# A three-stage fp32 kernel on one core: token sums of two blocks move to GpSimd, and kept products move ahead of a block's last units

## The chip, the cores and the metric

One core of a Trainium2 chip runs the whole program. The metric is the device time in microseconds of one execution, taken as the median over runs. Lower is better. The engines are TensorE (PE, with its weight loads as PEld), VectorE (DVE), ScalarE (ACT), GpSimd (POOL) and SyncE (SP), whose queue issues every DMA here.

## What is computed

Attention over 4 batches, 8 heads, 576 tokens and 64 columns (4 heads with a local mask, 4 with a strided one), then a maxout layer, then a second layer with a leaky activation:

```
x = attention(q, k, v)                                   # 2304 tokens x 512
x = max(x @ w1, x @ w2, x @ w3) @ w_out                  # 512 -> 768 -> 512
h = x @ w_in                                             # 512 -> 2048
out = (max(h, 0) + alpha * min(h, 0)) @ w_out2           # 2048 -> 512
```

## The kernel before, in words

Every fp32 operand of a matmul is kept as two parts, a high part (rounded to fp32r) and a low part (what the rounding left). A product is then three matmuls: high by high, low by high, high by low. `split` (L201) makes the two parts: the high one on ScalarE (L203), the low one by a subtraction (L206).

**First stage** (up to about 394 us). Attention and the maxout layer of batches 0 to 2 are written as tasks, and a planner (`Weave`) sets the order of the instructions. The maxout layer of the last batch is written by hand in `first_net`: 36 gate units of 12 matmuls each (L542), then 8 output units of 18 matmuls (L564). Its result goes to memory by the stores of L575.

**Second stage** (from about 395 us). The 2304 tokens are three blocks of 768, each block two halves of 384. Both products of the second layer are done with 7 block products where 8 would be usual, so sums and differences of the token rows are needed first. `load_x2` (L669) reads a half's rows, `sum_x2` (L677) makes four differences of 128x384, and `split_x2` makes high and low parts of the seven operands of that half. For block 0 this is done at the end of `first_net` and the parts stay on chip. For blocks 1 and 2 it is done early by the generator `early_x2`, whose parts are stored to memory (`xd`, L697) and fetched when the block begins (L704). The generator for block 1 runs beside `first_net`, one step in each of its 44 units `n`. The one for block 2 runs beside the pairs `n` = 1 to 15 of the second stage. In both, DVE does the differences and the low parts.

In the second stage a pair `n` (8 pairs `q` = 0 to 7 in a block) is seven products of the first matrix (`h_products`, L959) on two PSUM banks `ph`, `a` and `b_` in turn. DVE adds each bank up with what came before (L964) before the bank is written again. ACT and DVE then apply the activation (L916, L917, L920), make sums (L946) and split the four results `gts` (L795 on ACT, L796 on DVE). The products with the second matrix are units of 3 matmuls (`o_products`, L802): 12 units (`o_units`, `k` = 0 to 3, three units each) on six banks `po`, run one pair later between the `h_products`. Three more sums of each pair are kept (tiles `k`). After the last pair of a block their products are run: three groups `k` of eight pairs `p`, three units each (`kept_units`), which need `prepare` (split of a kept tile, ACT then DVE) first. `quarter` adds finished banks to the output and stores it.

Order around the block's end before: after the last `h_products` come two units of the pair before, then the nine units `k` = 0, 1, 2 of the last pair, then the kept products `p` = 0, 1 on the two `ph` banks, then the units `k` = 3, then all other kept products. `prepare` runs two ahead of its use:

```
for k in range(4):
    if q == NQ - 1 and k == 3:
        banks = [ps_h.tile(...) for _ in range(2)]
        for p in range(2):
            prepare(blk)
            yield from kept_units(blk, 0, p, banks, ...)
```

PSUM has eight banks. `ps_h` (two) is opened before `ps_o` (six), on the banks that `first_net` used.

Of the kernel before, what the change touches and what calls it, by code (L numbers as in the profile page):

```python
# [10 lines left out]
F32 = mybir.dt.float32  # L11
# [10 lines left out]
P = 128  # L22
# [19 lines left out]
NOW = 9  # L42

# [114 lines left out]
def attention_maxout_prelu_kernel(  # L158
# [523 lines left out]
    def split_x2(blk, k, i, pool, tag):  # L682

        t = pool.tile([P, 2, HB], F32R, tag=tag, name=tag)
        split(t[:, 0], t[:, 1], xs.pop((blk, PRODUCTS[k][1], i)), nc.scalar, nc.vector)
        return t

    def early_x2(blk, gap=0, rest=0):

        for i in range(2):  # L690
            rows = load_x2(blk, i, xsp, "xs")
            for _ in range(1 + gap):
                yield
            sum_x2(blk, i, rows, nc.vector)
            for k in range(7):
                t = split_x2(blk, k, i, xst, "xst")
                nc.sync.dma_start(xd[blk][k][i], t.bitcast(F32))  # L697
                for _ in range(1 + rest):
                    yield
# [53 lines left out]
    xst = pool(ctx, "xst", 2, "right")  # L753
    for n in range(2):
        load_h(n, (0, 2, 1, 3))
    early = early_x2(1, 2, 1)
    for n, _ in enumerate(first_net(B - 1, GATES_LAST)):
        if n in range(20, 32) and (n - 20) * 3 // 4 > (n - 21) * 3 // 4:
            load_ow()
        next(early, None)  # L760
        if n == LOAD_X:
            assert next(early, None) is None
# [5 lines left out]
        for i in range(2):  # L768
            if n == SPLIT_X + 2 * i:
                if i:  # L770
                    sum_x2(0, 1, rows[1], nc.vector)
                for k in range(7):
                    x2h[0, k, i] = split_x2(0, k, i, xmp, f"x{k}{i}")
# [7 lines left out]
    osp = pool(ctx, "osp", 3)  # L781
    ps_h = ctx.enter_context(tc.tile_pool(name="ps_h", bufs=2, space=PSUM, reuse_waits="tile"))
    ps_o = ctx.enter_context(tc.tile_pool(name="ps_o", bufs=6, space=PSUM, reuse_waits="tile"))
# [59 lines left out]
    def o_units(n):  # L843
        blk, q = divmod(n, NQ)
        for k in range(4):
            if q == NQ - 1 and k == 3:

                banks = [ps_h.tile([P, DM], F32, tag="ph", name="ph") for _ in range(2)]
                for p in range(2):
                    prepare(blk)  # L850
                    yield from kept_units(blk, 0, p, banks, parts_.pop((blk, 0, p)))
            w = words[blk, "o1", q, k // 2]
            for t in range(3):
# [10 lines left out]
                yield  # L864
        if q < NQ - 1:
            return
        for k in range(3):
            if k:
                banks = [ps_o.tile([P, DM], F32, tag="po", name="po") for _ in range(2)]
            for p in range(0 if k else 2, NQ):  # L870
                prepare(blk)
                yield from kept_units(blk, k, p, banks, parts_.pop((blk, k, p)))

    def kept_units(blk, k, p, banks, g):
        w = words[blk, "o2", k, p // 2]
        for t in range(3):
# [7 lines left out]
            while drains and (t == 2 or k == 2 and p == NQ - 1):  # L884
                quarter(*drains.pop(0))
                if len(drains) % 2 == 0 and p < NQ - 1:
                    break
# [60 lines left out]
    def h_products(n):  # L948
# [17 lines left out]
        a, b_ = banks  # L966
# [44 lines left out]
    early = early_x2(2)  # L1011
    outs = iter(())
    for n in range(NQ * NBLK):
# [9 lines left out]
        for i, _ in enumerate(h_products(n)):  # L1023
            if q == NQ - 1 and blk + 1 < NBLK:
                fetch_x2(blk + 1, i)
            if i == 0 and 0 < n < 16 and n != 8:
                for _ in range(2 if q in (5, 6) else 1):
                    next(early, None)
# [59 lines left out]
```

## Time and profile before

| what | value |
|---|---|
| median of 3 runs | 764.44 us (764.08 to 765.48) |
| profiled execution, first to last instruction | 762.9 us |
| around that span (median less span) | 1.5 us |
| PE busy | 741.8 us, 97% |
| DVE busy | 596.8 us, 78% |
| ACT busy | 454.7 us, 60% |
| POOL busy | 3.2 us, in 16 instructions |
| DMA | 199.37 MB, mean 261 GB/s |

The profiled execution's own time beside its span is not listed separately; the span is what the trace shows, and the sum in the prediction is made against it. Busy shares are averages over the stages. PE's is modelled from pipelined matmuls, so that small waits between weight loads can hide in it: counts of matmuls over a stretch say more than the busy time.

### The profile page before, as it was taken

How to read it: one execution, taken by the hardware profiler on the slowest of the kernel's cores; microseconds unless marked ns; L12 is line 12 of the kernel's file. 1: busy time of each engine (PE TensorE's matmuls, PEld its weight loads, DVE VectorE, ACT ScalarE, POOL GpSimd, SP SyncE). 2: the span in 40 equal slices, each digit the busy share in tenths (PEclk: the TensorE clock that was granted, in tenths of full speed). 3: DMA queues.
4: the chain of work that ended last, by engine and by line, in shares of the span. 5: the costliest groups of instructions: out<-in, count | busy, mean ns of one | idle time of the engine just before them, and what ended most of it. 6: DMA issues, size and time to landing. Idle time of an engine off the chain costs nothing.

```text
span 762.9 us, 16093 instructions
## 1 busy us (share of the span) xinstructions
PE 741.8 (97%) x5704; PEld 723.0 (95%) x5704; DVE 596.8 (78%) x1670; ACT 454.7 (60%) x1226; POOL 3.2 (0%) x16
## 2 busy tenths in 40 slices
PE   5899999999999999999999999999999999999997
PEld 4699999999999999999999999999999999999997
DVE  5999999888777987336368988878888877888894
ACT  6988897756665775323246566624666644566561
POOL 1000000000000000000000000000000000000000
PEclk9699999999999999999999999999999999999999
DMA  7387769877878856566938889999888999878361
GB/s 245 130 259 232 240 216 326 271 273 255 300 248 282 270 202 213 171 259 192 362 113 285 273 289 320 386 403 334 291 285 301 354 401 328 273 239 259 121 194 59
DMA packets 85471, 199.37 MB, mean 261 GB/s; under 512 B 10640, under 2 KB 40848, under 8 KB 85392
## 3 DMA queue, kind: packets, MB, share of 16 engines
q1 hardware_dynamic: 85392, 198.35, 75.9%
q8 instruction: 45, 0.74, 0.4%
q14 instruction: 34, 0.28, 0.1%
HBM read 148.51 MB, written 49.81 MB: 260 GB/s over the span
## 4 chain that ended last, share of the span: by engine, by line
PE 77%; DVE 12%; DMA 5%; ACT 2%; issue 2%; SPq 1%; DVEq 0%; ACTq 0%
PE bank L542 27%; PE ph L959 20%; PE po L802 15%; PE bank L564 9%; PE bank L314 3%; PE bank L380 2%; PE bank L355 2%; DVE g L796 2%; DVE c L806 2%; DMA w<-wh 1%; DMA w<-wp 1%; DVE e L322 1%; DMA xs<-x 1%; DMA x<-xd 1%; DVE c L964 1%
## 5 line engine op out<-in xcount | busy, mean ns | idle before, releaser
L542 PE MATMUL bank<-x,w 128*128 128x288 f32 x1728 | 236.5, 297 | 0.3 <-DVE t L553 0.3
L542 PEld LDWEIGHTS bank<-x,w 128*128 128x128 f32 x1728 | 231.1, 189 | 2.1 <-DVE t L553 0.6
L959 PE MATMUL ph<-x,w 128*128 128x384 f32 x1008 | 203.4, 337 | 1.8 <-DVE c L964 1.2
L802 PE MATMUL po<-w,g 128*128 128x256 f32 x1296 | 183.8, 282 | 1.7 <-DVE g L796 0.8
L802 PEld LDWEIGHTS po<-w,g 128*128 128x128 f32 x1296 | 175.4, 189 | 4.2 <-DVE g L796 3.2
L959 PEld LDWEIGHTS ph<-x,w 128*128 128x128 f32 x1008 | 168.3, 188 | 3.0 <-DVE c L964 1.9
L964 DVE TENSOR_TENSOR c<-ph,c 128x384 f32<-128x384 f32 x168 | 91.0, 554 | 32.7 <-PE ph L959 31.8
L795 ACT CAST g<-c 128x384 fp32r<-128x384 f32 x96 | 48.5, 505 | 89.7 <-DVE c L946 53.0
L564 PE MATMUL bank<-h,w 128*128 128x288 f32 x576 | 79.9, 297 | 0.4 <-DVE nm L322 0.4
L564 PEld LDWEIGHTS bank<-h,w 128*128 128x128 f32 x576 | 76.9, 188 | 1.8 <-DVE nm L322 0.8
L250 DVE TENSOR_TENSOR w<-word,w 128x512 fp32r<-128x512 f32 x88 | 55.4, 637 | 23.9 <-ACT w L247 23.5
L329 ACT ACTIVATE e<-e,nm 96x128 f32<-96x128 f32 (+2 forms) x176 | 68.0, 394 | 6.0 <-DVE nm L322 6.0
L916 ACT ACTIVATE c<-c 128x384 f32<-128x384 f32 x96 | 50.5, 526 | 33.9 <-DVE c L964 32.9
L247 ACT CAST w<-word 128x512 fp32r<-128x512 f32 x88 | 50.6, 582 | 32.0 <-DMA wh<-w 17.7
L917 ACT ACTIVATE c<-c,nalpha 128x384 f32<-128x384 f32 x96 | 59.2, 617 | 3.1
L920 DVE SCALAR_TENSOR_TENSOR c<-c 128x384 f32<-128x384 f32 x96 | 53.0, 552 | 9.0 <-ACT c L917 9.0
L796 DVE TENSOR_TENSOR g<-c,g 128x384 fp32r<-128x384 f32 x96 | 52.9, 551 | 1.9 <-ACT g L795 1.9
L796 DVE TENSOR_TENSOR g<-k,g 128x384 fp32r<-128x384 f32 x72 | 36.8, 550 | 14.4 <-ACT g L795 14.4
L439 ACT ACTIVATE word<-raw 128x512 f32<-128x512 f32 x56 | 37.4, 677 | 11.5 <-DMA raw<-in_w 5.9
L445 DVE SCALAR_TENSOR_TENSOR word<-raw,word 128x512 uint32<-128x512 uint32 x56 | 38.8, 693 | 1.9
L631 DVE TENSOR_TENSOR t<-bank,t 128x288 f32<-128x288 f32 x72 | 32.6, 452 | 7.8 <-PE bank L542 7.1
L795 ACT CAST g<-k 128x384 fp32r<-128x384 f32 x72 | 33.4, 515 | 7.8 <-PE po L802 4.4
(72 smaller groups left out, 679.8 us busy)
## 6 DMA issues: line engine op xcount, KB each, us to landing
w<-wh SPq DMA_DIRECT2D x72, 512.0 KB, 5.0
raw<-in_w SPq DMA_DIRECT2D x50, 512.0 KB, 4.5
w<-wo SPq DMA_DIRECT2D x48, 512.0 KB, 5.9
w<-wp SPq DMA_DIRECT2D x36, 512.0 KB, 6.3
wh<-w SPq DMA_DIRECT2D x24, 512.0 KB, 3.7
xd<-xst SPq DMA_DIRECT2D x28, 384.0 KB, 3.5
x<-xd SPq DMA_DIRECT2D x28, 384.0 KB, 8.1
wp<-w SPq DMA_DIRECT2D x24, 256.0 KB, 3.0
```

The lines of the kernel that those rows point to most:

```text
L247: (nc.scalar.copy if e == "ACT" else nc.vector.tensor_copy)(out_, in_)
L250: nc.vector.tensor_tensor(out=out_, in0=x, in1=y, op=ALU.subtract)
L329: nc.scalar.activation(tl[ek][:nq, j, i, :nk], tl[ek][:nq, j, i, :nk], AF.Exp, bias=tl["nm", u][:nq, j, i:i + 1], scale=-1.0, accum_out=tl ...
L542: nc.tensor.matmul(acc, words["gate", f, g][:, wi, cc * P:(cc + 1) * P], xt[b, cc, hf][:, xi, :], start=n == 0, stop=n == 3 * NCC - 1)
L564: nc.tensor.matmul(acc, words["mix", f][:, wi, dc * P:(dc + 1) * P], st["h", hf, f][:, xi, :], start=n == 0, stop=n == 3 * NF1 - 1)
L795: nc.scalar.copy(g[:, 0], x)
L796: return g, lambda: nc.vector.tensor_tensor(out=g[:, 1], in0=x, in1=g[:, 0].bitcast(F32), op=ALU.subtract)
L802: nc.tensor.matmul(bank[:, NH * half:NH * (half + 1)], g[:, gi, t * P:(t + 1) * P], w[:, wi, off:off + NH], start=first and i == 0, stop=l ...
L917: nc.scalar.activation(a, a, AF.Copy, scale=nalpha[:, f:f + 1])
L920: nc.vector.scalar_tensor_tensor(out=a, in0=h, scalar=0.0, in1=a, op0=ALU.max, op1=ALU.add)
L959: nc.tensor.matmul(bank, words["h", n, i][:, wi, off + c * P:off + (c + 1) * P], x2h[blk, k, c][:, xi, :], start=m == 0, stop=m == 5)
L964: nc.vector.tensor_tensor(out=out_, in0=bank, in1=other, op=ALU.add)
```

## The change

1. The differences and low parts of blocks 1 and 2 go from DVE to GpSimd (`lo_engine=nc.gpsimd`, `sum_x2(..., nc.gpsimd)`). High parts stay on ACT. They are 16 differences and 28 low parts, each 128x384.
2. The rows of both halves of block 1 are loaded ahead of the first eight weight loads `wh`, the second half into a pool `xr` of its own.
3. The steps of both blocks stand in tables by `n`, and the store of a part is issued a step later than its split.
4. For block 0 the second half's differences and splits are written one unit apart.
5. `ps_o` is opened before `ps_h`, and the seven products begin on the other bank (`b_, a = banks`).
6. The kept products `p` = 0, 1 run ahead of all twelve units of the last pair. `prepare` then runs after units 1, 2 and 3, and up to five ahead (`AHEAD`). Finished banks are added at most two at a time.

```diff
+EARLY = 6
-    def split_x2(blk, k, i, pool, tag):
+    def split_x2(blk, k, i, pool, tag, lo_engine=nc.vector):
-        split(t[:, 0], t[:, 1], xs.pop(...), nc.scalar, nc.vector)
+        split(t[:, 0], t[:, 1], xs.pop(...), nc.scalar, lo_engine)
-    def early_x2(blk, gap=0, rest=0):
...
+    def early_load(blk, i, pool, tag):
+        early_rows[blk, i] = load_x2(blk, i, pool, tag)
+    def early_sums(blk, i):
+        sum_x2(blk, i, early_rows.pop((blk, i)), nc.gpsimd)
+    def early_split(blk, i, k):
+        early_parts.append((blk, k, i, split_x2(blk, k, i, xst, "xst", nc.gpsimd)))
+    def early_store():
+        for blk, k, i, t in early_parts:
+            nc.sync.dma_start(xd[blk][k][i], t.bitcast(F32))
+        early_parts.clear()
...
+    xrp = pool(xrx, "xr", 2, "right")
+    early_load(1, 0, xsp, "xs")
+    early_sums(1, 0)
+    early_load(1, 1, xrp, "xr")
     for n in range(2):
         load_h(n, (0, 2, 1, 3))
-    early = early_x2(1, 2, 1)
+    ready = {EARLY + 19 * j // 10: divmod(j, 7) for j in range(14)}
     for n, _ in enumerate(first_net(B - 1, GATES_LAST)):
-        next(early, None)
+        if n - 1 in ready:
+            early_store()
+        if n in ready:
+            if ready[n] == (1, 0):
+                early_sums(1, 1)
+            early_split(1, *ready[n])
...
-    ps_h = ctx.enter_context(tc.tile_pool(name="ps_h", bufs=2, ...))
     ps_o = ctx.enter_context(tc.tile_pool(name="ps_o", bufs=6, ...))
+    ps_h = ctx.enter_context(tc.tile_pool(name="ps_h", bufs=2, ...))
...
     def o_units(n):
+        if q == NQ - 1:
+            first = [ps_h.tile([P, DM], F32, tag="ph", name="ph") for _ in range(2)]
+            for p in range(2):
+                yield from kept_units(blk, 0, p, first, parts_.pop((blk, 0, p)))
         for k in range(4):
-            if q == NQ - 1 and k == 3:
...
+            if q == NQ - 1 and k > 0:
+                prepare(blk)
...
             for p in range(0 if k else 2, NQ):
-                prepare(blk)
+                for _ in range(1 if k == 0 or p == 0 else 2):
+                    if len(parts_) < AHEAD:
+                        prepare(blk)
...
-        a, b_ = banks
+        b_, a = banks
...
-    early = early_x2(2)
+    early = {1: [(0, None)], 2: [(0, 0)], 3: [(0, 1)], 4: [(0, 2)], 5: [(0, 3), (0, 4)], 6: [(0, 5)], 7: [(0, 6)],
+             9: [(1, None)], 10: [(1, 0)], 11: [(1, 1), (1, 2)], 12: [(1, 3)], 13: [(1, 4), (1, 5)], 14: [(1, 6)]}
```

**PE at the end of block 0** (`ph<-x` are the seven products, `po` and `ph<-w,g` the products with the second matrix; 3 matmuls are one unit). Before:

```order
L959 MATMUL ph<-x_5716,w 128x384 x3
L959 MATMUL ph<-x_5790,w 128x384 x3
L802 MATMUL po<-w,g 128x256 x33
L802 MATMUL ph<-w,g 128x256 x18
L802 MATMUL po<-w,g 128x256 x9
L802 MATMUL ph<-w,g 128x256 x54
L802 MATMUL po<-w,g 128x256 x36
```

And now:

```order
L977 MATMUL ph<-x_5720,w 128x384 x3
L977 MATMUL ph<-x_5817,w 128x384 x3
L816 MATMUL po<-w,g 128x256 x6
L816 MATMUL ph<-w,g 128x256 x18
L816 MATMUL po<-w,g 128x256 x36
L816 MATMUL ph<-w,g 128x256 x54
L816 MATMUL po<-w,g 128x256 x36
```

The 18 matmuls of kept products moved 27 matmuls forward; the total is the same.

**DVE at the same place** (`g<-c,g` is the low part of the last of the four results, `g<-k,g` low parts of kept tiles, L806 and L820 the output additions). Before:

```order
L796 TENSOR_TENSOR g<-c,g 128x384
L946 TENSOR_TENSOR k<-c 128x384 x2
L796 TENSOR_TENSOR g<-k,g 128x384 x2
L806 TENSOR_TENSOR c_7158<-po,m_7138 128x256
L796 TENSOR_TENSOR g<-k,g 128x384
L806 TENSOR_TENSOR c_7183<-po,m_7140 128x256
```

And now:

```order
L810 TENSOR_TENSOR g<-c,g 128x384
L964 TENSOR_TENSOR k<-c 128x384 x2
L810 TENSOR_TENSOR g<-k,g 128x384 x5
L820 TENSOR_TENSOR c_7196<-po,m_7176 128x256
L810 TENSOR_TENSOR g<-k,g 128x384
L820 TENSOR_TENSOR c_7210<-po,m_7178 128x256
```

Five kept tiles are split ahead of the first output addition, where two were.

**DVE in pair 2**, at the first differences of block 2 (`xs`, `t`, `xst`). Before:

```order
L796 TENSOR_TENSOR g<-c,g 128x384
L677 TENSOR_TENSOR t<-xs 128x384
L677 TENSOR_TENSOR xs<-xs 128x384
L677 TENSOR_TENSOR t<-xs 128x384
L677 TENSOR_TENSOR t<-xs,t 128x384
L206 TENSOR_TENSOR xst<-xs,xst 128x384
L964 TENSOR_TENSOR c<-ph,c 128x384
L946 TENSOR_TENSOR k<-c 128x384
```

And now on DVE:

```order
L810 TENSOR_TENSOR g<-c,g 128x384
L982 TENSOR_TENSOR c<-ph,c 128x384
L964 TENSOR_TENSOR k<-c 128x384
L964 TENSOR_TENSOR c<-k,c 128x384
```

The five rows left DVE; they stand on POOL's queue, the four differences one pair earlier (beside pair 1).

## Rows read from the trace of the kernel before

**Rows 1.** The page's head: span, and each engine's busy time, share and instructions.

```profile
span 762.9 us, 16093 instructions
PE 741.8 (97%) x5704; PEld 723.0 (95%) x5704; DVE 596.8 (78%) x1670; ACT 454.7 (60%) x1226; POOL 3.2 (0%) x16
```

**Rows 2.** Stretches: length, PE, PEld, DVE, ACT, POOL busy (instructions), PE clock, DMA share, GB/s.

```profile
422.00:484.00 62.00, 62.00 (x419) 61.95 (x418) 54.05 (x111) 39.41 (x79) 0.00 (x0) 1.00 0.90 309
485.23:504.79 19.56, 19.00 (x151) 18.19 (x151) 17.48 (x42) 9.46 (x22) 0.00 (x0) 1.00 1.03 401
606.17:625.74 19.57, 19.01 (x152) 18.19 (x151) 17.48 (x42) 9.45 (x22) 0.00 (x0) 1.00 1.03 401
```

**Rows 3.** PE in time order, end of block 0: start, length, instruction, [idle before, releaser].

```profile
485.23 2.55 PE L802 MATMUL po<-w,g 128*128 128x256 f32 x17
487.94 2.58 PE L802 MATMUL po<-w,g 128*128 128x256 f32 x16 [0.15 <-DVE g L796]
...
493.59 6.64 PE L802 MATMUL ph<-w,g 128*128 128x256 f32 x54
500.07 2.56 PE L802 MATMUL po<-w,g 128*128 128x256 f32 x20
...
504.79 1.22 PE L959 MATMUL ph<-x,w 128*128 128x384 f32 x6
```

**Rows 4.** PE in time order, end of block 2, the last block.

```profile
726.31 2.55 PE L802 MATMUL po<-w,g 128*128 128x256 f32 x17
...
743.86 15.26 PE L802 MATMUL po<-w,g 128*128 128x256 f32 x124
```

**Rows 5.** PE in time order, its other waits after 330 us.

```profile
337.72 38.38 PE L542 MATMUL bank<-x,w 128*128 128x288 f32 x288 [0.32 <-DVE t L553]
...
395.82 6.52 PE L959 MATMUL ph<-x,w 128*128 128x384 f32 x36 [0.67 <-ACT xo L651]
...
421.09 1.32 PE L959 MATMUL ph<-x,w 128*128 128x384 f32 x6 [0.49 <-DVE c L964]
...
530.47 1.32 PE L959 MATMUL ph<-x,w 128*128 128x384 f32 x6 [0.41 <-DVE c L964]
```

**Rows 6.** DVE in time order, end of block 0.

```profile
491.05 0.56 DVE L796 TENSOR_TENSOR g<-c,g 128x384 fp32r<-128x384 f32 x1 [0.63 <-ACT g L795]
491.53 1.02 DVE L946 TENSOR_TENSOR k<-c 128x384 f32<-128x384 f32 x2
492.46 1.02 DVE L796 TENSOR_TENSOR g<-k,g 128x384 fp32r<-128x384 f32 x2
```

**Rows 7.** SP's queue at the start of the last batch's maxout layer.

```profile
325.12 3.04 SPq L669 DMA_DIRECT2D xs<-x  x4
```

**Rows 8.** DVE in time order: differences of block 1, then of block 2 in pair 2.

```profile
334.50 0.56 DVE L677 TENSOR_TENSOR t<-xs 128x384 f32<-128x384 f32 x1 [9.92 <-DMA xs<-x]
...
417.77 0.55 DVE L677 TENSOR_TENSOR t<-xs 128x384 f32<-128x384 f32 x1
...
420.02 0.55 DVE L206 TENSOR_TENSOR xst<-xs,xst 128x384 fp32r<-128x384 f32 x1
```

**Rows 9.** ACT in time order: the last two groups of output copies of `first_net`.

```profile
392.87 1.29 ACT L651 COPY xo<-bank 128x288 f32<-128x288 f32 x4
395.36 0.40 ACT L651 COPY xo<-bank 128x288 f32<-128x288 f32 x1 [1.21 <-DMA x<-xo]
```

**Rows 10.** Groups by line and shape: instruction xcount | busy us, mean ns | idle before us, releasers.

```profile
L964 DVE TENSOR_TENSOR c<-ph,c 128x384 f32<-128x384 f32 x168 | 91.0, 554 | 32.7 <-PE ph L959 31.8
L920 DVE SCALAR_TENSOR_TENSOR c<-c 128x384 f32<-128x384 f32 x96 | 53.0, 552 | 9.0 <-ACT c L917 9.0
L796 DVE TENSOR_TENSOR g<-c,g 128x384 fp32r<-128x384 f32 x96 | 52.9, 551 | 1.9 <-ACT g L795 1.9
L946 DVE TENSOR_TENSOR k<-c 128x384 f32<-128x384 f32 x72 | 37.6, 550 | 0.0
L196 POOL TENSOR_SCALAR_AFFINE_SELECT mask_s<-mask_s 128x126 f32<-128x126 f32 x1 | 0.3, 337 | 0.1
```

More of the change, by code (lines that the diff above doesn't have):

```diff
@@ L680, in sum_x2 @@
             xs[blk, name, i] = x
-    def split_x2(blk, k, i, pool, tag):
+    def split_x2(blk, k, i, pool, tag, lo_engine=nc.vector):
         t = pool.tile([P, 2, HB], F32R, tag=tag, name=tag)
-        split(t[:, 0], t[:, 1], xs.pop((blk, PRODUCTS[k][1], i)), nc.scalar, nc.vector)
+        split(t[:, 0], t[:, 1], xs.pop((blk, PRODUCTS[k][1], i)), nc.scalar, lo_engine)
         return t
-    def early_x2(blk, gap=0, rest=0):
[L690 to L699, printed above, removed]
+    early_rows, early_parts = {}, []
+    def early_load(blk, i, pool, tag):
[8 more added lines that the diff above has]
+        early_parts.clear()
     def fetch_x2(blk, k):
@@ L767, in attention_maxout_prelu_kernel @@
             xmp = pool(ctx, "xmp", 1, "right")
[L768 to L773, printed above, removed]
+        if n == SPLIT_X + 1:
+            sum_x2(0, 1, rows[1], nc.vector)
+        for i, ks in {0: [(0, range(7))], 2: [(1, range(4))], 3: [(1, range(4, 7))]}.get(n - SPLIT_X, []):
+            for k in ks:
+                x2h[0, k, i] = split_x2(0, k, i, xmp, f"x{k}{i}")
     xx.close()
@@ L781, in attention_maxout_prelu_kernel @@
     osp = pool(ctx, "osp", 3)
+    ps_o = ctx.enter_context(tc.tile_pool(name="ps_o", bufs=6, space=PSUM, reuse_waits="tile"))
     ps_h = ctx.enter_context(tc.tile_pool(name="ps_h", bufs=2, space=PSUM, reuse_waits="tile"))
[L783 removed]
     NH = DM // 2
@@ L867, in o_units @@
         for k in range(3):
-            if k:
-                banks = [ps_o.tile([P, DM], F32, tag="po", name="po") for _ in range(2)]
+            banks = [ps_o.tile([P, DM], F32, tag="po", name="po") for _ in range(2)] if k else first
             for p in range(0 if k else 2, NQ):
-                prepare(blk)
+                for _ in range(1 if k == 0 or p == 0 else 2):
+                    if len(parts_) < AHEAD:
+                        prepare(blk)
                 yield from kept_units(blk, k, p, banks, parts_.pop((blk, k, p)))
+    AHEAD = 5
     def kept_units(blk, k, p, banks, g):
@@ L883, in kept_units @@
                 load_ow()
[L884 to L887, printed above, removed]
+            last = k == 2 and p == NQ - 1
+            if t == 2 or last:
+                for _ in drains[:] if last else drains[:2]:
+                    quarter(*drains.pop(0))
             yield
@@ L1025, in attention_maxout_prelu_kernel @@
                 fetch_x2(blk + 1, i)
-            if i == 0 and 0 < n < 16 and n != 8:
-                for _ in range(2 if q in (5, 6) else 1):
-                    next(early, None)
+            if i == 0:
+                for half, k in early.get(n, ()):
+                    if k is None:
+                        early_load(2, half, xsp, "xs")
+                        early_sums(2, half)
+                    else:
+                        early_split(2, half, k)
+            if i == 3:
+                early_store()
             for _ in range(units_before[i + 1] - units_before[i]):
```

7 lines of the change are left out of this document (3 added, 4 removed).

## The prediction, made before the changed kernel was run

> **What bounds the kernel now.** I read the page's head first: TensorE is busy 741.8 of 762.9 us, VectorE 596.8, GpSimd 3.2 [rows 1]. The change removes no matmul, so all it can give back is time in which PE waits. The reader should not stop at the 21 us that "97% busy" leaves, for two reasons. Part of it lies in attention at the start and in the last additions and stores, which the change leaves alone. And the busy time is modelled, so that a wait between two matmuls can count as busy. So I next read PE in order of time and compared how long a stretch takes with its number of matmuls.
>
> At the end of block 0 the 54 matmuls of kept products that begin at 493.59 take until 500.07, which is 6.48 / 54 = 0.120 us each without a wait [rows 3]. From 485.23 to 504.79 stand 33 + 18 + 9 + 54 + 36 = 150 such matmuls, 18.00 us at that pace. They take 19.56: **1.56 us lost**, although the busy column says only 0.56 [rows 2, 3]. The second block's stretch is 19.57, so 1.57 lost [rows 2]. In the last block 134 matmuls stand from 726.31 to 743.86: 17.55 less 16.08 is 1.47 lost [rows 4]. Together 4.6 us. The row at 487.94 names the wait: the low part of a split on VectorE.
>
> PE's other waits behind 330 us are four: 0.32, 0.67, 0.49 and 0.41 us, 1.89 in all [rows 5]. So what the change can win is about 4.6 + 1.9 = 6.5 us and a little in the last group of products, 124 matmuls in 15.26 us where 14.88 would do [rows 4]. With that 0.4 the ceiling is 6.9.
>
> **The kept products moved ahead.** After the last seven products, PE has six matmuls of the pair before, until 485.23 + 0.72 = 485.95. Then came the last pair's units at once, whose gates were not split yet. Now 18 matmuls of kept products come first, whose operands were prepared two products earlier. They fill 2.16 us. So the units begin at 488.11, the second three (27 matmuls behind 485.95) at 489.19. The old order had the operand of these by 487.94 [rows 3], so this wait goes. The fourth three begin 45 matmuls behind 485.95, at 491.35. Their low part is used by the third matmul, at 491.59, and VectorE finishes it at 491.05 + 0.56 = 491.61 [rows 6]. That is 0.02 late. The third three use a low part that is earlier in VectorE's order, so I give it no wait.
>
> What is late next is the first kept product behind the units. It begins at 492.43 and its third matmul wants a low part at 492.67. VectorE has two subtractions (491.53) in front of it and starts it at 492.46, done at 493.01 [rows 6]: 0.34 late. After that five low parts run back to back, at about 0.47 each (two take 1.02, one 0.55), while PE needs 1.08 us for each, so VectorE gets ahead. The six additions of finished banks that came in one burst are now spread two banks at a time. I see no wait behind it, until the next block's first product. By this count 0.36 of the 1.56 stays, and the gain is 1.20 + 1.21 + 1.11 = **3.5 us**. Its bounds are 4.6 (nothing stays) and 1.2 (the wait only moves behind the filled 2.16 us, with 0.4 won in each block).
>
> **Rows first, and VectorE freed in the maxout layer.** VectorE stood 9.92 us waiting for rows [rows 8], as the first difference was in its queue ahead of the layer's maxima. PE lost 0.32 in the end, because eight banks cover the rest. On GpSimd that wait holds nobody. Gain **0.3 us**. The eight row loads that now stand ahead of the eight weight loads on SP take 3.04 / 4 = 0.76 us each to issue [rows 7], so the weights start some 6 us later, and they are first used at 395.82 [rows 5]. I cost that at nothing. The store of each part stands one step behind its split; SP waits there for GpSimd, with weight loads queued behind it, which were issued two pairs (over 20 us) ahead of their use.
>
> **The bank swap.** The first product at 395.82 waits 0.67 for an output copy on ACT [rows 5]. That is the very last copy, which itself waited 1.21 for an earlier store [rows 9]: the first `ph` bank is the bank of the last output unit. With the pools opened the other way round, and the other bank first, it is the bank of the unit before, whose copy is among the four from 392.87 to 394.16. Done a microsecond before PE needs it. Gain **0.7 us** (bounds 0 and 0.7).
>
> **Differences and low parts of block 2.** The waits at 421.09 and 530.47 come from VectorE's additions being late [rows 5]. In front of the first stand the four differences and a low part, from 417.77 to 420.5, 2.8 us at one stretch [rows 8]. These leave VectorE, which saves 22 operations of some 0.5 us in this stage. From 422 to 484 us PE ran 419 matmuls in 62.00 us; a pair has 42 + 36 = 78, so it takes 11.5 us, of which VectorE is busy 54.05 / 62.00, 10.0 us, with one low part or two among them, about 9.5 without [rows 2]. That leaves 2 us of slack in a pair.
>
> What the 44 operations cost on GpSimd, no row shows. Below stands 0.55 us, VectorE's own time [rows 10]. The nearest row on GpSimd is a one-input operation of 126 columns in 0.337 us: three times the width makes 1.0 us, and if two inputs are read one after the other 2.0 us [rows 10]. I take 1.0. The Trainium skill (GPSIMD Engine Reference, Performance versus the Vector engine) measures 4497 ns for a two-input add of 2048 columns; an estimate from it is 0.84 us, by which the sum would be the same. The work has no consumer nearby: in the maxout layer the parts come 1.9 units apart (about 3 us), in the second stage one or two in a pair of 11.5 us. So at 1.0 us the duration is hidden, and its cost is nothing unless it holds VectorE (a rival below). Of the 0.49 + 0.41 I take **0.6 us**, since the differences of 4.0 us run beside a full VectorE. Bounds: 0.9, and a loss as in that rival.
>
> **Sum.** 3.5 + 0.3 + 0.7 + 0.6 = 5.1 us off the profiled span of 762.9: 757.8. The median of the runs stands 1.5 us above the span (764.44), so I forecast **759.3 us**.
>
> **Rivals.**
> 1. **The wait at a block's end moves instead of going.** VectorE is busy 17.48 of 19.56 us there [rows 2], and does the same operations as before; reordering does not shorten it. If its queue behind the fill holds PE again, 0.4 per block is won, 1.2, and the differences' 0.6 may fail as well. With 0.3 and 0.7 that is 2.2 us: **762.2**. Against it: over the 19.56 us VectorE has 2 us idle, and five low parts ahead are more than the two before.
> 2. **GpSimd holds VectorE.** Suppose a GpSimd operation that reads two tiles makes VectorE's operations with two SBUF inputs wait until it ends. At least 11 of some 18 in a pair are such (four each of L920 and L796, three of L946, against seven L964 that read a PSUM bank) [rows 10]. Four differences of D each then take 4D from a pair with 2.0 us of slack. At D = 1.0 each of the two bursts stalls PE by 2.0, 4.0 in place of the 0.9: 4.5 won elsewhere less 3.1 is 1.4, so **763.0**, no change. At D = 1.5 the bursts cost 8.0, and the three pairs with two low parts 1.0 each: 11.0 against 5.4 won, so **770**. It becomes slower from D of about 1.1. The Trainium skill has this as a rule (SBUF — State Buffer, Who interferes with whom): the two share a read interface, and the later one waits for the whole instruction. No run so far shows it, since GpSimd is idle once VectorE is busy. Against the full price: the other operations, and VectorE's idle 2 us, run on beside it, and two operations in turn do not hold each other longer than one.
> 3. **The change does nothing to PE**, because its waits are covered by other releasers that come at the same time (a weight load, the kept tiles). Then **764.4**. For it speaks only that the waits are short; each row names VectorE or ACT as the last releaser.
>
> **How the numbers follow.** The forecast's own case (757.6 to 761) gets 0.62. Rival 1 gets 0.20 (761 to 763). Rival 2 at no change together with rival 3 gets 0.11, rival 2 at a loss 0.07. A difference of 0.2%, 1.5 us, is about what a measurement of this kernel can tell from none, so faster is below 762.9 and slower above 766.0. Faster: 0.62 + 0.17 of rival 1 + 0.04 of the third = 0.83. Same: 0.10. Slower: 0.07. The range goes from the ceiling, 764.44 - 6.9 = 757.5, up to the upper end of rival 1, 762.9: that holds about 0.62 + 0.17 + 0.03.
>
> **What would show it.** Right: from the first unit behind the last seven products to the next block's first product 18.3 to 18.6 us instead of 19.56; no wait of PE at about 395, and 0.1 or less where it was 0.32; VectorE's busy time down by some 22 us (44 operations), GpSimd's up to about 47. GpSimd's differences at 1.0 us each. Wrong: `c<-ph` additions of VectorE late in pairs 2 and 9, or L920 and L796 lengthened beside GpSimd (rival 2); a wait on `g<-k` of the usual size at the first kept product behind the units (rival 1). The forecast fails if GpSimd needs 2 us per operation.

## The result, and the profile after

The changed kernel takes 759.01 us (median of 6 runs, 757.04 to 760.17) against 764.64 us (6 runs, 763.17 to 768.91) of the kernel before on the same chip: a ratio of 0.9915, interval 0.9891 to 0.9938. Times 764.64 that is 6.5 us faster, 4.7 to 8.3 (the medians as such differ by 5.6). The profiled execution took 757.04 us, 2.0 more than its span.

The page's head of the changed kernel, which answers to [rows 1]:

```profile
span 755.0 us, 16154 instructions
PE 737.7 (98%) x5704; PEld 721.6 (96%) x5704; DVE 587.0 (78%) x1626; ACT 455.1 (60%) x1226; POOL 51.0 (7%) x60
```

The span is 7.9 us shorter. Not all of it is the change: the last batch's maxout layer begins at 316.83 instead of 318.20, and up to there PE, DVE and ACT have the same instructions in both. In the profiles of this study that start lies between 316.72 and 319.65, whatever the kernel, which also explains most of the scatter of the totals. Behind it, stretches repeat within some 0.4 us (pairs 0, the widest, take 88.40 to 88.82 in runs with the same work there; why is told below). So I compare stretches, cut at the starts of rows in PE's order of time ("layer": from the layer's first matmul to the first product `ph<-x`; "pairs" and "end": a block to its last product, and from there to the next block's first one, in block 2 to the last matmul's end).

| kernel | layer | pairs 0 | end 0 | pairs 1 | end 1 | pairs 2 | end 2 |
|---|---|---|---|---|---|---|---|
| before | 77.62 | 89.41 | 19.56 | 101.38 | 19.57 | 100.57 | 32.81 |
| changed | 76.16 | 88.44 | 18.49 | 100.62 | 18.49 | 100.57 | 31.63 |
| won | 1.46 | 0.97 | 1.07 | 0.76 | 1.08 | 0.00 | 1.18 |

The row "won" sums to 6.52 us, as much as the ratio says. Half of it, 3.33, is at the three ends.

PE of the changed kernel in order of time: the layer and the first products, then the end of block 0 (answers to [rows 3, 5]).

```profile
316.83 57.28 PE L543 MATMUL bank<-x,w 128*128 128x288 f32 x432
373.95 19.20 PE L565 MATMUL bank<-h,w 128*128 128x288 f32 x144
392.99 6.41 PE L977 MATMUL ph<-x,w 128*128 128x384 f32 x36
...
481.42 0.88 PE L816 MATMUL po<-w,g 128*128 128x256 f32 x6
482.14 2.36 PE L816 MATMUL ph<-w,g 128*128 128x256 f32 x18
484.33 4.64 PE L816 MATMUL po<-w,g 128*128 128x256 f32 x36
488.80 6.96 PE L816 MATMUL ph<-w,g 128*128 128x256 f32 x54
495.60 4.48 PE L816 MATMUL po<-w,g 128*128 128x256 f32 x36
499.92 1.22 PE L977 MATMUL ph<-x,w 128*128 128x384 f32 x6
```

The layer runs 432 + 144 matmuls without a named wait, and the first product follows without one (it was 0.67). The end takes 18.50 for the 150 matmuls that need 18.00. Of what is left, 0.32 sits where the 54 matmuls of kept products begin (6.80 us to the next row instead of 6.48) and 0.15 in the 36 matmuls of the units ahead of them (4.47 instead of 4.32).

PE's idle column shows no wait there, but the weight loads do. PEld at the first of these places:

```profile
488.69 0.31 PEld L816 LDWEIGHTS ph<-w,g 128*128 128x128 f32 x2
489.27 6.29 PEld L816 LDWEIGHTS ph<-w,g 128*128 128x128 f32 x52 [0.27 <-DVE g L810]
```

Two weight loads pass, and the third waits 0.27 us for a low part.

The view that I should have read from the start is the waits of PEld, here from 335 us to the end (engine, tile and line, releaser: us in total, times, longest). Before:

```profile
PEld po L802 <- DVE g L796: 3.2, 9, 0.4
PEld ph L959 <- DVE c L964: 1.9, 3, 0.7
PEld po L802 <- ACT g L795: 0.9, 3, 0.3
PEld ph L959 <- ACT xo L651: 0.9, 1, 0.9
PEld bank L542 <- DVE t L553: 0.6, 1, 0.6
```

Changed:

```profile
PEld ph L816 <- DVE g L810: 0.8, 3, 0.3
PEld ph L977 <- DVE c L982: 0.6, 1, 0.6
```

7.5 us became 1.4. By place: the ends 3.2 + 0.9 to 0.8, 3.3 less (3.33 in the table); the layer and its seam 0.9 + 0.6 to nothing, 1.5 (table 1.46); the products of the pairs 1.9 to 0.6, 1.3 (table 0.97 + 0.76 = 1.73). Each is within 0.5 of what the stretches show.

VectorE lost 44 operations and only 9.8 us (596.8 to 587.0), not the 22 that I forecast for them. The groups of the changed kernel over the whole run answer to [rows 10]:

```profile
L982 DVE TENSOR_TENSOR c<-ph,c 128x384 f32<-128x384 f32 x168 | 90.9, 553 | 39.2 <-PE ph L977 38.2 <-ACT xst L204 0.2
L938 DVE SCALAR_TENSOR_TENSOR c<-c 128x384 f32<-128x384 f32 x96 | 54.7, 570 | 8.6 <-ACT c L935 8.6
L810 DVE TENSOR_TENSOR g<-c,g 128x384 fp32r<-128x384 f32 x96 | 54.7, 570 | 1.9 <-ACT g L809 1.9
L964 DVE TENSOR_TENSOR k<-c 128x384 f32<-128x384 f32 x72 | 40.4, 588 | 0.0
L964 DVE TENSOR_TENSOR c<-k,c 128x384 f32<-128x384 f32 x24 | 15.5, 645 | 0.8
```

The additions that read one PSUM bank and one SBUF tile keep their 553 ns. Four groups with two SBUF inputs went from between 550 and 558 to between 570 and 645, 8.4 us in all; the fifth, `g<-k,g`, stays at 550, at the ends, where GpSimd is idle. In the last maxout layer twelve low parts `h` of 128x288 went from 459 to 716, 3.1 us. There the difference went. Where it happens is seen in pair 1, beside the first differences on GpSimd. POOL, then DVE, in order of time:

```profile
324.41 1.01 POOL L678 TENSOR_TENSOR t<-xs 128x384 f32<-128x384 f32 x1 [320.16 <-DMA xs<-x]
...
406.64 1.45 POOL L678 TENSOR_TENSOR t<-xs 128x384 f32<-128x384 f32 x1 [35.60 <-DMA xs<-x]
408.16 1.22 POOL L678 TENSOR_TENSOR xs<-xs 128x384 f32<-128x384 f32 x1
...
410.75 1.31 POOL L678 TENSOR_TENSOR t<-xs,t 128x384 f32<-128x384 f32 x1
```

```profile
407.64 0.85 DVE L810 TENSOR_TENSOR g<-c,g 128x384 fp32r<-128x384 f32 x1
408.42 1.37 DVE L938 SCALAR_TENSOR_TENSOR c<-c 128x384 f32<-128x384 f32 x1
409.71 1.01 DVE L982 TENSOR_TENSOR c<-ph,c 128x384 f32<-128x384 f32 x2
...
411.58 0.90 DVE L938 SCALAR_TENSOR_TENSOR c<-c 128x384 f32<-128x384 f32 x1
```

Both are held: GpSimd's difference is 1.01 where it is alone and 1.22 to 1.45 here; three operations of VectorE take 0.85, 1.37 and 0.90 instead of 0.55, 1.47 more in all. Each of the three ends 0.40 to 0.42 us after a GpSimd instruction has ended: 408.49 behind 408.09, 409.79 behind 409.38, 412.48 behind 412.06 (start plus length of the rows). So it waits for the rest of that instruction, up to 0.82, and then runs. In the second stage 19 operations of VectorE with two SBUF inputs of 384 columns take over 0.62 us, and all 19 end so. `c<-ph` in between keeps its pace. This is the mechanism of rival 2.

The rule of the Trainium skill (SBUF — State Buffer, Who interferes with whom) is that the two engines share a read interface and the later one waits for the other's whole instruction. The trace agrees with it.

The pair had 2 us of slack, and in this trace PE does not notice. That is not so in every run with the same work here. In two runs below, "rows behind" and "both", a `c<-ph` addition behind the held operations comes too late, and PE's weight load waits 0.35 us for it, which makes pairs 0 88.8 instead of 88.4. In "rows behind":

```profile
412.12 0.99 PEld L977 LDWEIGHTS ph<-x,w 128*128 128x128 f32 x6 [0.35 <-DVE c L982]
```

### The profile page after: what moved, and what is told of

It reads as the page before. It is cut to its first block, busy times and chain, and to the rows that moved or that the text cites. A ratio compares the mean times of both kernels' runs of the same rounds, so it can differ in the third digit from the quotient of the medians.

```text
span 755.0 us, 16154 instructions
## 1 busy us (share of the span) xinstructions
PE 737.7 (98%) x5704; PEld 721.6 (96%) x5704; DVE 587.0 (78%) x1626; ACT 455.1 (60%) x1226; POOL 51.0 (7%) x60
## 4 chain that ended last, share of the span: by engine, by line
PE 83%; DVE 7%; ACT 5%; DMA 4%; issue 1%; SPq 0%; DVEq 0%; ACTq 0%
PE bank L543 23%; PE ph L977 23%; PE po L816 19%; PE bank L565 9%; PE ph L816 3%; PE bank L315 2%; DMA raw<-in_w 2%; PE bank L381 2%; PE bank L356 2%; ACT e L330 1%; DMA raw<-in_wo 1%; DVE word L446 1%; ACT word L440 1%; DVE e L323 1%; DVE e L263 1%
## 5 line engine op out<-in xcount | busy, mean ns | idle before, releaser
L816 PE MATMUL po<-w,g 128*128 128x256 f32 x1296 | 181.1, 281 | 0.0
L938 DVE SCALAR_TENSOR_TENSOR c<-c 128x384 f32<-128x384 f32 x96 | 54.7, 570 | 8.6 <-ACT c L935 8.6
L810 DVE TENSOR_TENSOR g<-c,g 128x384 fp32r<-128x384 f32 x96 | 54.7, 570 | 1.9 <-ACT g L809 1.9
L964 DVE TENSOR_TENSOR k<-c 128x384 f32<-128x384 f32 x72 | 40.4, 588 | 0.0
```

The lines of the kernel that those rows point to most:

```text
L810: return g, lambda: nc.vector.tensor_tensor(out=g[:, 1], in0=x, in1=g[:, 0].bitcast(F32), op=ALU.subtract)
L816: nc.tensor.matmul(bank[:, NH * half:NH * (half + 1)], g[:, gi, t * P:(t + 1) * P], w[:, wi, off:off + NH], start=first and i == 0, stop=l ...
L938: nc.vector.scalar_tensor_tensor(out=a, in0=h, scalar=0.0, in1=a, op0=ALU.max, op1=ALU.add)
```

## The experiments

All start from the changed kernel. The stretches of each, by the cuts of the table above, and its time (the median for "changed", "three kept" and "VectorE, loads ahead", one run for the others, with the scatter of the start in it):

| run | layer | pairs 0 | end 0 | pairs 1 | end 1 | pairs 2 | end 2 | time |
|---|---|---|---|---|---|---|---|---|
| changed | 76.16 | 88.44 | 18.49 | 100.62 | 18.49 | 100.57 | 31.63 | 759.01 |
| units first | 76.16 | 88.40 | 19.15 | 100.81 | 19.17 | 100.57 | 32.29 | 759.73 |
| old drains | 76.16 | 88.46 | 18.97 | 100.62 | 18.97 | 100.58 | 32.10 | 759.41 |
| both | 76.16 | 88.81 | 19.17 | 100.62 | 19.17 | 100.57 | 32.28 | 760.23 |
| two ahead | 76.16 | 88.44 | 18.50 | 101.13 | 18.52 | 100.88 | 31.63 | 760.00 |
| three kept | 76.16 | 88.41 | 18.50 | 100.74 | 18.50 | 100.57 | 31.62 | 759.19 |
| banks back | 76.86 | 88.68 | 18.50 | 100.71 | 18.50 | 100.56 | 31.64 | 757.94 |
| rows behind | 76.16 | 88.82 | 18.50 | 100.79 | 18.51 | 100.58 | 31.62 | 758.57 |
| VectorE | 76.17 | 95.07 | 18.50 | 110.08 | 18.51 | 100.57 | 31.63 | 774.23 |
| VectorE, loads ahead | 76.16 | 89.29 | 18.51 | 100.93 | 18.50 | 100.57 | 31.63 | 760.44 |
| six more | 76.16 | 90.93 | 20.00 | 104.64 | 25.96 | 100.57 | 31.63 | 773.12 |
| twelve more | 76.16 | 91.54 | 26.30 | 105.84 | 24.92 | 102.59 | 31.62 | 783.53 |
| writes only | 76.16 | 88.70 | 19.33 | 100.57 | 18.51 | 102.54 | 31.62 | 762.26 |

### What won at the ends of the blocks

**Units first**: the kept products `p` = 0, 1 stand before `k` = 3 again.

```diff
-        if q == NQ - 1:
-            first = [...]
-            for p in range(2):
-                yield from kept_units(blk, 0, p, first, ...)
         for k in range(4):
+            if q == NQ - 1 and k == 3:
+                first = [...]
+                for p in range(2):
+                    yield from kept_units(blk, 0, p, first, ...)
```

> Only the order at a block's end is undone: the last pair's units 0 to 2 run first, then the two kept products, then unit 3; prepare still runs ahead and GpSimd keeps its work. My theory (the 2.16 us of kept products cover the splits of the last pair): the stretch from the first of these units to the next block's first product, 18.50 us in the changed kernel and 19.56 before, goes back by 0.9 to 1.2 us per block to about 19.2 to 19.5, with the wait of some 0.3 us on a low part back at the second three units; some 3 us more in all, about 761 to 762. Rival (running prepare ahead and adding two banks at a time brought the gain, the order did not): the stretch stays at 18.7 or less, and the whole within 0.5 us of the changed kernel.

The ends lose 0.66, 0.68 and 0.66 us, 2.0 of the 3.3 and less than the theory asked. Some 0.4 per block stays won without the order. What holds that?

**Old drains**, alone and **both** together:

```diff
-            last = k == 2 and p == NQ - 1
-            if t == 2 or last:
-                for _ in drains[:] if last else drains[:2]:
-                    quarter(*drains.pop(0))
+            while drains and (t == 2 or k == 2 and p == NQ - 1):
+                quarter(*drains.pop(0))
+                if len(drains) % 2 == 0 and p < NQ - 1:
+                    break
```

> The changed kernel with the rule of before for finished banks (added until an even number is left, instead of at most two at a time); all else as changed. It asks for the 0.41 us per block's end which stayed won when the order of the kept products was undone. Theory: that 0.41 is the burst of additions in front of low parts on VectorE, so the ends of blocks 0 and 1 take 18.8 to 19.0 us instead of 18.50. Rival: the 0.41 came from splits that are issued between the last pair's units, and with the kept products ahead the burst is covered: 18.50 stays.

> The units of the last pair first again (as in the run that undid the order) and the old rule for finished banks with it; only the splits between the last units and up to five ahead stay from the change. Theory (the burst of additions was the 0.41): the ends go from 19.15 to about 19.55 us, as in the kernel before. Rival (the splits between the units were): they stay at 19.15.

With the kept products ahead, the old rule costs 0.48 per end. PE in order of time in that run, and then VectorE:

```profile
500.56 1.10 PE L816 MATMUL po<-w,g 128*128 128x256 f32 x7 [0.21 <-DVE g L810]
```

```profile
499.63 0.41 DVE L820 TENSOR_TENSOR c<-ph,m 128x256 f32<-128x256 f32 x1
499.96 2.42 DVE L810 TENSOR_TENSOR g<-k,g 128x384 fp32r<-128x384 f32 x5
```

Nothing but additions stands on VectorE from 496.64 to 499.96, and PE waits for the low part behind them. So the theory of the first of these runs held. In the second it fell: with the units first the same rule costs 0.02 (19.15 to 19.17). The two are not terms of a sum: the order without the new rule is worth 0.20 (19.17 to 18.97), the rule without the order nothing, both 0.68 (19.17 to 18.49). The remaining 0.39 of 1.07 (19.56 to 19.17) must then come from the splits that are issued between the last pair's units, or further ahead. That is by elimination; undoing the place of these splits was not tried. The weight loads show which wait went with it: before, one stood in the last 36 matmuls of an end, and with both undone these run through. PEld before, and in "both":

```profile
502.78 1.97 PEld L802 LDWEIGHTS po<-w,g 128*128 128x128 f32 x16 [0.35 <-DVE g L796]
```

```profile
497.61 4.39 PEld L816 LDWEIGHTS po<-w,g 128*128 128x128 f32 x36
```

**Two ahead**: `prepare` one at a time, two kept tiles ahead of use instead of five.

```diff
-            if q == NQ - 1 and k > 0:
+            if q == NQ - 1 and k > 1:
                 prepare(blk)
...
-                for _ in range(1 if k == 0 or p == 0 else 2):
-                    if len(parts_) < AHEAD:
-                        prepare(blk)
+                prepare(blk)
```

> Only the running ahead of prepare is undone: two tiles ahead in place of up to five. The order of units and the rest stay. My theory (the burst of additions held the low parts of the third group of kept products, 0.3 to 0.4 us per block): the stretch of 36 matmuls ahead of the next block's first product, 4.32 us in the changed kernel and 4.72 before, goes back to 4.5 to 4.7; some 0.5 to 1 us in all. Rival (order alone was enough): the stretch stays 18.5 and nothing changes. A third outcome is that the first kept product behind the units waits less, because fewer low parts stand in VectorE's queue.

The ends do not move, so my expectation failed: running ahead as such is not what wins there. What it gives is behind the end, 0.5 and 0.3 us in the next block's pairs.

**Three kept**: three kept products ahead of the units instead of two.

```diff
-            for p in range(2):
+            for p in range(3):
...
-            for _ in range(2):
+            for _ in range(3):
                 prepare(blk)
...
-            for p in range(0 if k else 2, NQ):
+            for p in range(0 if k else 3, NQ):
```

> Three kept products run ahead of the last pair's units in place of two (27 matmuls, 3.24 us, and three tiles prepared in the last of the pairs). My theory: what is left of the wait at a block's end is 0.3 us per block at the first kept product behind the units, because two subtractions stand ahead of its low part; one more product of 1.08 us ahead covers that, and the stretch falls from 18.5 to 18.0 to 18.2, so 0.9 to 1.4 us in all, about 758. Rival (the third split in the last pair delays its own gates on ACT and VectorE by 0.5 us each): the wait goes to the fourth three units, and nothing is won.

Nothing is won, as the rival had it: 18.50, and the median of 759.19 us is a ratio of 0.9918 (0.9889 to 0.9947) to before, the changed kernel's own within the noise. But the wait went elsewhere than the rival said. The first kept product behind the units now runs without one; the first kept product ahead of them waits instead. PEld, then VectorE:

```profile
484.06 0.76 PEld L816 LDWEIGHTS ph<-w,g 128*128 128x128 f32 x6 [0.27 <-issue]
484.98 2.57 PEld L816 LDWEIGHTS ph<-w,g 128*128 128x128 f32 x21 [0.15 <-DVE c L982]
```

```profile
482.02 1.50 DVE L810 TENSOR_TENSOR g<-k,g 128x384 fp32r<-128x384 f32 x3 [0.71 <-ACT g L809]
483.44 0.55 DVE L982 TENSOR_TENSOR c<-ph,c 128x384 f32<-128x384 f32 x1
```

The kept products write the two `ph` banks of the last seven products, and each bank is free when a `c<-ph` addition has read it. The third split stands ahead of these additions on VectorE. The first ends at 483.99, and the weight load begins at 484.06. The profile names no releaser for that wait; for the next one, at 484.98, it names the second addition. So two products ahead fit what VectorE can split in time, and three do not.

### The seam of the layer

**Banks back**: `ps_h` opened before `ps_o`, and the products begin with the other bank, as before.

```diff
-    ps_o = ...
     ps_h = ...
+    ps_o = ...
...
-        b_, a = banks
+        a, b_ = banks
```

> Only the banks are undone: the two-bank pool is opened first and the seven products begin on the first bank. My theory: PE waits 0.5 to 0.7 us for the last output copy at about 393, as before; at a block's end the first kept product now needs the bank of the last of the seven products, which VectorE frees 0.5 to 0.7 us after it is done, so that 0.2 to 0.6 more is lost in each block; in all 1 to 2.5 us. Rival (rows that arrive earlier had already freed ACT): no wait at 393, and no change at the block's end.

The layer takes 0.70 us more, and PE waits again for the last output copy:

```profile
393.58 6.52 PE L977 MATMUL ph<-x,w 128*128 128x384 f32 x36 [0.53 <-ACT xo L652]
```

The ends stay as they are; there I had expected a loss and was wrong.

**Rows behind**: the row loads of block 1 stand behind the first weight loads again.

```diff
-    early_load(1, 0, xsp, "xs")
-    early_sums(1, 0)
-    early_load(1, 1, xrp, "xr")
     for n in range(2):
         load_h(n, (0, 2, 1, 3))
+    early_load(1, 0, xsp, "xs")
+    early_sums(1, 0)
+    early_load(1, 1, xrp, "xr")
```

> Only SP's order is undone: the eight weight loads go ahead of the row loads of block 1; GpSimd keeps its work. My theory (what counts is that VectorE no longer waits for rows, not when they land): GpSimd's first difference begins some 8 us later, at about 333, PE has no wait in the last maxout layer, the time does not change by more than 0.5 us outside attention. Rival (the rows' early arrival matters): ACT's high parts wait for the rows, its copies of PE's banks come late, and PE waits 0.3 us or more before 345.

The layer keeps 76.16. On GpSimd the wait for rows holds nobody, wherever the loads stand.

### GpSimd or VectorE

**VectorE**: the early work back on VectorE at its new places.

```diff
-        sum_x2(blk, i, early_rows.pop((blk, i)), nc.gpsimd)
+        sum_x2(blk, i, early_rows.pop((blk, i)), nc.vector)
...
-        early_parts.append((..., split_x2(blk, k, i, xst, "xst", nc.gpsimd)))
+        early_parts.append((..., split_x2(blk, k, i, xst, "xst", nc.vector)))
```

> Only the engine is undone: the differences and low parts of blocks 1 and 2 are on VectorE again, at the changed kernel's places in the program. My theory: PE's waits in pairs 2 and 9 or 10 come back at 0.4 to 0.6 us each, and a wait of 0.3 in the last maxout layer, since VectorE again waits for rows; the time from the first product of the second stage to the end, 362.0 us in the changed kernel, grows by 0.9 to 1.7. Rival (GpSimd holds VectorE as long as the work took there): VectorE's L938, L810 and L964 groups fall back to 0.55 us each, and PE's time does not grow; it may shrink.

The layer keeps 76.17 here too: rows first alone would have been enough for it, as GpSimd alone was. But the pairs lose 6.6 and 9.5 us, where my theory had 0.9 to 1.7 in all and the rival none. PE and VectorE in order of time:

```profile
412.19 2.29 PE L977 MATMUL ph<-x,w 128*128 128x384 f32 x6 [4.93 <-DVE c L982]
```

```profile
409.34 0.56 DVE L678 TENSOR_TENSOR t<-xs 128x384 f32<-128x384 f32 x1 [3.88 <-DMA xs<-x]
```

In the new table rows are loaded in the pair of their differences, and VectorE takes its queue in order, so that the DMA's time becomes PE's. The waits of the weight loads account for 12.1 of the 16.1 us (12.7 in this run, 0.6 in the changed kernel). The rest fits TensorE's clock: at PE's waits of 4.93 and 6.82 us the granted clock fell to 0.50 (1.2 instead of 2.4 GHz), from 412.04 to 415.45 and from 534.91 to 545.15, and six matmuls take 2.29 us there instead of 1.21. PE was busy for 8.6 us of these two stretches; half of that, 4.3, is my estimate of what the clock took. None of this is a price of the engine; the next run shows that one.

**VectorE, loads ahead**: the same, with the loads one and two pairs ahead of the differences as before the change.

```diff
-    early = {1: [(0, None)], 2: [(0, 0)], ..., 7: [(0, 6)],
-             9: [(1, None)], ...
+    early = {1: [(0, "load")], 2: [(0, "sums"), (0, 0)], ..., 7: [(0, 6), (1, "load")],
+             9: [(1, "sums")], ...
...
```

> The changed kernel with the differences and low parts of blocks 1 and 2 on VectorE again, and the row loads of block 2 issued as early as before the change (the first half one pair, the second two pairs ahead of its differences). The run with this work on VectorE at the new places lost 16 us because loads and differences stood in the same pair; here that is gone, so this run prices the engine alone. Theory: the move to GpSimd is worth only the waits of TensorE at the start of pairs 2 and 9, so from the first product to the end of block 0's pairs 88.9 to 89.5 us instead of 88.44, block 1's pairs 101.1 to 101.5 instead of 100.62, together 1.0 to 1.8 us, and the maxout layer's end stays at 76.16 (rows first is enough there). Rival: GpSimd's reads lengthen VectorE by as much as the move saves, so the engine does not matter: both stretches within 0.2 us of the changed kernel. Second rival: VectorE's slack is gone at the new places, over 3 us lost.

The median is 760.44 us (12 runs) against 764.75 (17 runs) of before: a ratio of 0.9942 (0.9924 to 0.9959), so 0.9942 x 764.75 = 760.3, 4.4 us faster (3.1 to 5.8) with none of the early work on GpSimd. Pairs 0 take 0.85 more than with the change and pairs 1 0.31, 1.16 in all. The sum is inside the theory's 1.0 to 1.8; pairs 1 with 100.93 are less than the 101.1 that it asked, and pairs 0 scatter by 0.4. By the medians this run wins 2.1 us less than the change (4.4 against 6.5), with intervals that overlap and the scatter of the start in them. PE's wait in pair 2 is the old one, to the hundredth:

```profile
420.98 1.32 PE L977 MATMUL ph<-x,w 128*128 128x384 f32 x6 [0.49 <-DVE c L982]
```

So the move between engines is worth some 1.2 us of the 6.5.

### How far GpSimd holds VectorE

**Six more**, **twelve more**: 6 or 12 extra subtractions of 128x256 on GpSimd in each pair, on a tile of their own. **Writes only**: 27 fills of that tile instead, which read nothing.

```diff
...
+    i0 = idle.tile([P, DM // 2], F32, name="i0")
...
+            if i == 1 and n > 0:
+                for _ in range(6):          # or 12
+                    nc.gpsimd.tensor_tensor(out=i0, in0=i0, in1=i0, op=ALU.subtract)
+                for _ in range(27):         # in writes only
+                    nc.gpsimd.memset(i0, 0.0)
```

> Six operations of 128x256 with two inputs in SBUF are added on GpSimd in each pair 1 to 23 (some 0.7 us each alone, 4 us a pair); nothing reads their result. If GpSimd holds VectorE's two-input operations, as their lengthening beside GpSimd in the changed kernel (up to 1.37 us in place of 0.55) suggests: the mean of L938, L810 and L964 rises by 0.1 us or more, VectorE's busy time by 1.5 to 3 us a pair. With some 2 us of slack a pair PE then waits by up to 1 us a pair, 0 to 20 us in all. If it does not hold it: VectorE's means stay, and the time stays within 0.5 us.

> The same with twelve operations, 8 us of GpSimd in a pair of 11.5. If held: twice the lengthening, 3 to 6 us a pair, more than the slack of 2, so 1 to 4 us a pair are lost and the whole is 20 to 90 us slower. If not held: no change, since GpSimd still has time and nobody waits for it but the parts of block 2.

> In place of the six operations with two inputs, 27 memsets of the same 128x256 tile in each pair (some 0.3 us each, 8 us a pair, as long as the twelve operations take). If it is GpSimd's reading that holds VectorE: VectorE's means stay at the changed kernel's, and the time does too, within 1 us. If any GpSimd access holds it: a loss like that of the twelve operations.

Groups between 400 and 600 us. The changed kernel:

```profile
L982 DVE TENSOR_TENSOR c<-ph,c 128x384 f32<-128x384 f32 x105 | 56.7, 552 | 19.1 <-PE ph L977 18.6 <-ACT xst L204 0.2
L938 DVE SCALAR_TENSOR_TENSOR c<-c 128x384 f32<-128x384 f32 x60 | 34.9, 581 | 5.1 <-ACT c L935 5.1
```

Six more:

```profile
L985 DVE TENSOR_TENSOR c<-ph,c 128x384 f32<-128x384 f32 x102 | 54.7, 548 | 5.8 <-PE ph L980 5.6
L941 DVE SCALAR_TENSOR_TENSOR c<-c 128x384 f32<-128x384 f32 x59 | 40.8, 692 | 7.7 <-ACT c L938 7.6
```

Twelve more:

```profile
L985 DVE TENSOR_TENSOR c<-ph,c 128x384 f32<-128x384 f32 x97 | 51.9, 547 | 6.2 <-PE ph L980 6.1
L941 DVE SCALAR_TENSOR_TENSOR c<-c 128x384 f32<-128x384 f32 x56 | 43.6, 779 | 4.0 <-ACT c L938 3.9
```

Writes only:

```profile
L1059 POOL MEMSET i<- 128x256 f32 x367 | 114.6, 312 | 20.3
L985 DVE TENSOR_TENSOR c<-ph,c 128x384 f32<-128x384 f32 x106 | 57.5, 554 | 18.8 <-PE ph L980 17.7 <-ACT xst L204 0.4
L941 DVE SCALAR_TENSOR_TENSOR c<-c 128x384 f32<-128x384 f32 x60 | 38.0, 633 | 3.9 <-ACT c L938 3.9
```

I summed what the five groups of VectorE with two SBUF inputs of 384 columns took above the means that they have in the changed kernel. Six more: 20.6 us beside 72.5 us more of GpSimd, 0.28 for each. Twelve more: 31.6 beside 119.7, 0.26. Writes only: 3.0 beside 113, 0.03. The additions `c<-ph`, with one SBUF input, stay between 547 and 554 ns everywhere. So it is reading by both that holds them, not GpSimd's being busy. Even the 0.03 is not the fills': 231 of these operations ran beside fills alone, and took 543 to 567 ns. All 17 that take over 0.62 us in "writes only" stand beside the kernel's own differences and low parts, which fall on other operations there (the `k<-c` group, 611 in the changed kernel, is at 550; the two groups shown are longer).

The price for PE is not in proportion. Pairs lose up to 5 us, but the ends up to 8: with six more, end 1 grows from 18.49 to 25.96, a place where VectorE was busy 17.48 of 19.56 us before [rows 2]. PE there, and the busy times and the granted clock (third number from the end) of a stretch that begins just before:

```profile
622.06 9.16 PE L819 MATMUL ph<-w,g 128*128 128x256 f32 x52 [1.32 <-DVE g L813]
```

```profile
621.33:628.16 6.83, 6.10 (x28) 6.10 (x29) 6.83 (x11) 2.95 (x7) 6.20 (x9) 0.50 0.98 376
```

52 matmuls take 9.16 us, where 54 took 6.96 in the changed kernel. PE had waited 1.22, 0.47 and 1.32 us between 617 and 622, and the granted clock was at 0.50 (1.2 GHz) for 6.83 us. PE was busy for 6.10 of them; half of that, 3 of the 7.5 us lost, is my estimate of what the clock took. With twelve more the same level stands from 498.38 to 505.21, at end 0. So a wait on VectorE can cost PE more than its length.

Writes only lost 0.8 at end 0 and 2.0 in the last pairs, and so missed the 1 us that I had allowed. In the last pairs PE waits 1.72 us for a weight load (`w<-wp`), at end 0 0.44 at the first kept product; why these come late is open.

## Why the prediction was right, and where it was not

The forecast of 759.3 us, in a range of 757.5 to 762.9, met 759.01, and its chance for "faster" was 0.83. By its steps:

- **The ends** [rows 3, 4]: 3.5 forecast, 3.33 measured; each takes 18.49 where I wrote 18.3 to 18.6. The wait that I put at 0.34 us, third matmul of the first kept product behind the units, stands at the third weight load there with 0.27. The count of matmuls times their pace was the right way to the size. The share of causes was not: I credited the order, yet the order alone is worth 0.20 to 0.66, depending on the rule for finished banks, and 0.39 comes from elsewhere: it is the wait at 502.78, which the count held but no row named, and which the order does not touch. The step that failed is to put that count down to the order. That the additions "are now spread two banks at a time" was a side remark, and is worth 0.48.
- **The bank swap** [rows 9]: 0.7 forecast, 0.70 by the run that undid it.
- **Rows first, VectorE freed in the layer**: 0.3 forecast; 1.46 less 0.70 leaves 0.76. The step that failed is taking the size of a wait from PE's idle column [rows 5], 0.32 there; its weight loads wait 0.6 for the same releaser. Either half of the change, rows first or GpSimd, gives it alone.
- **Differences and low parts of block 2**: 0.6 forecast, 1.73 measured in pairs 0 and 1. Here too the idle column (0.49, 0.41) was too small, and the bound of 0.9 with it. Of the 1.73 the engine accounts for 1.16; the other 0.57 is not traced to one part of the change.
- **GpSimd's duration**: 1.0 us taken, 1.01 measured alone, 1.22 to 1.45 beside VectorE's reads. That the first is so near is luck: the nearest row was an operation of another kind, and nothing decided between 1.0 and 2.0.
- **VectorE down by 22 us**: wrong, 9.8. The step that failed is "its cost is nothing unless it holds VectorE", for it does hold VectorE. I had this mechanism as rival 2, and priced it too high: four differences were to hold VectorE by 4.0 us, and held it by 1.47, since only three operations with two SBUF inputs met them, each for the rest of one instruction, and `c<-ph` additions run on in between. So it stayed within the 2 us of slack that I had counted. In the changed kernel's trace it cost PE nothing; in "rows behind" and "both" it cost 0.35.
- **Sum**: 5.1 forecast, 6.5 measured. The span was to be 757.8 and is 755.0, of which 1.37 is the earlier start and 1.4 the terms that were too small. That the median lies within 0.3 us of the forecast all the same is partly chance: six runs scatter by 3 us.

Rival 1 (the wait moves) shows only its 0.27 us. Rival 3 is out: every wait named went with its releaser.

No variant's stretches sum to less than the changed kernel's 434.40 us; three kept comes nearest with 434.50. Behind 335 us PEld waits 1.4 us in all, so little is left to win there.

## What to carry to other kernels

Size PE's short waits by the matmuls of a stretch times their pace, and by the waits of its weight loads; the idle column of the matmuls alone had about half of them or less in three of four places here. Work handed to GpSimd is not free for VectorE: each microsecond of GpSimd's reading added about a quarter of one to VectorE's operations with two SBUF inputs, so it pays where VectorE has that slack, and beside a full VectorE it cost several microseconds, in part, by my estimate, because the granted clock of TensorE fell at the waits. And an engine that takes its queue in order must not stand behind a load issued in the same step: the same move back to VectorE cost 16 us with the load beside it (some 4 of them, by my estimate, to the clock) and 1.2 with the loads one and two pairs ahead.

## What was unexpected of the hardware

- GpSimd and VectorE slow each other: 1.01 to 1.45 us for a difference of 128x384, 0.55 to 1.37 for one operation of VectorE. A held operation of VectorE ends some 0.41 us after GpSimd's instruction has ended (19 of 19 in the changed kernel, 172 of 172 with twelve more). With a PSUM bank as one input VectorE's addition is not touched (means of 547 to 554 ns in every run).
- GpSimd's fills of 128x256 (0.31 us each, 114.6 us in a stretch of 200) cost VectorE nothing: 543 to 567 ns for its operations with two SBUF inputs beside them.
- TensorE's granted clock fell to 0.50 at single waits of PE: for 3.4 us at one of 4.9, for 6.8 us at three of 0.5 to 1.3 in a row. The matmuls there take longer as well (six of 128x384 2.29 us instead of 1.21), so such a wait is paid twice.
- Two edits at one place were worth 0.68 us together, and 0.20 and nothing each without the other.
